# One product for y of a half chunk over v's tokens and the state's rows, in an RWKV-5 and SoLU feed-forward kernel

## The chip, the core and the metric

The kernel runs on one core of one Trainium2 chip. The metric is device time in microseconds (us); the kernel before takes 344.68 us (median of 3 runs, 343.82 to 345.14).

The core's engines have a queue each and run side by side, held together by semaphores: TensorE (PE: matmuls; PEld are its weight loads), VectorE (DVE), ScalarE (ACT), GpSimd (POOL), and SyncE (SP), which here issues nearly all DMAs. SBUF is the on-chip memory of 128 partitions, PSUM the accumulator memory that TensorE writes.

## The reference

```python
# attention: B=4, H=8, S=768, D=48, float32
for t in range(S):
    kt, vt, rt = (k[:, :, t], v[:, :, t], r[:, :, t])
    cur = np.einsum('bhd,bhe->bhde', u[None] * kt, vt)
    y[:, :, t] = np.einsum('bhd,bhde->bhe', rt, state + cur)
    state = w[None, :, :, None] * state + np.einsum('bhd,bhe->bhde', kt, vt)
# feed-forward: x is y as (3072 tokens, 384), d_ff = 1024
h = x @ w_in
e = np.exp(h - h_max); sm = e / (np.sum(e) + 1e-09); solu = h * sm
ln = (solu - mean) / np.sqrt(var + 1e-06) * g_ln
return ln @ w_out
```

The recurrence over tokens is computed in chunks. Within a chunk y is a masked product of scores (r against k, decayed) with v, plus a diagonal term (u), plus the product of r with the state carried in.

## The kernel before

A chunk is 128 tokens of one batch: 24 chunks, in the order batch fastest, so chunk i and chunk i+4 belong to the same batch. `direct_path` is written out by hand in the order in which every engine's instructions are issued; each engine runs its own in that order, and a later one can't pass an earlier one that waits. A general path behind a flag isn't run with these inputs.

Chunks 0 to 6 (`i < WHOLE`) are handled whole: `whole_scores`, `whole_y`, `whole_outer`. From chunk 7 on a chunk is cut in two halves of 64 tokens (`U`), and the main loop (`for i in range(LA + LO, ...)`) takes two chunks a turn; its first turn, i = 7, has an order of its own (`late`). In a turn with chunks i and i+1, and with the feed-forward of older chunks (ffn_in of j = i-2 and j+1, ffn_out of l = i-7 and l+1), TensorE's order is:

ffn_in(j), within(i, i+1), ffn_out(l), carried(i), carried(i+1), ffn_in(j+1), ffn_out(l+1), scores(i+2, i+3), outer(i+2, i+3).

The pieces that the change and the prediction touch:

- `diagonal` (L729): ScalarE writes for each of 8 heads the unit matrix times the diagonal term into AT; `take_scores` (L788): VectorE copies the masked scores over it, per chunk 2 instructions of 128x256.
- `scores` (L781) into two PSUM banks, `outer` (L880) into two buffers of the PSUM pool psM, which has four; psM also serves o_ps of ffn_out (L1016) and y_ps of the whole chunks.
- `within` (L843): y from AT and v, 32 products of 64 rows x 32 columns a chunk, into the two score banks. `carried` (L854) adds r times the state (first half) or times the state in mid chunk (second half), 24 products of 128 rows x 32 columns a chunk. The profile counts each float32 product twice, as two records.
- `take_y` (L864): ScalarE copies y out of PSUM into xT, the operand of ffn_in (L926) of the same chunk, which runs in the next turn.
- `middle` (L898): VectorE makes the state in mid chunk. `update` (L910, L914): VectorE adds the second half's outer product, GpSimd multiplies by the decay.
- `ffn_in` (L926) writes h into the one buffer of psH; ScalarE takes exp (L931); `unit` has VectorE's reciprocal (L937) and product solu (L939), which releases h, and ScalarE's identity (L941) and square (L942).
- `halve_ln` (L977), `halve_k` (L989), `halve_r` (L994): copies that split 32-bit words into halves, so that a transposing DMA on SP's queue (L966) can turn them; `join_ln` and `join_rk` (both L971) are VectorE's copies that put the words together again as lnT and rk.
- `decay_k`, `decay_r`, `weigh` (L697, L704, L710, L711): GpSimd's preparation of k, r and the diagonal term; `sum_own` (L715) is VectorE's sum for the latter.
- `check_next`: ScalarE's mag (L563) and VectorE's least (L565), a check of one piece of the weights a turn.
- `load`: k, r and v by three DMAs of SP a chunk (L472).

Of the kernel before, what the change touches and what calls it, by code (L numbers as in the profile page):

```python
# [399 lines left out]
def direct_path(  # L400
# [29 lines left out]
    nc = tc.nc  # L430
# [35 lines left out]
    kpads = [const.tile([128, H, P], F32, name=f"kpad{i}") for i in range(NLD)]  # L466
    vts = [const.tile([128, H, D + 32], F32, name=f"vt{i}") for i in range(NV)]
    def load(i, which="krv"):
        b, c = units[i]
        for t, src, n in ((kpads, k, "k"), (rpads, r, "r"), (vts, v, "v")):  # L470
            if n in which:
                nc.sync.dma_start(out=t[i % len(t)][:, :, 0:D],  # L472
                                  in_=src[b, :, ts(c, T), :].rearrange("h s d -> s h d"))


# [15 lines left out]

    banks = [psA.tile([128, HP * T], F32, name=f"at{q}") for q in range(2)]
    for ps in banks:
# [102 lines left out]
    for vt in vts:  # L596
        nc.gpsimd.memset(vt[:, :, D:], 0.0)
    neg_half = const.tile([128, 1], F32, name="neg_half")
    nc.gpsimd.memset(neg_half, -0.5)


    states = [const.tile([128, HP, 2, D], F32, name=f"state{b}") for b in range(B)]
    for St in states:
        nc.scalar.activation(out=St.rearrange("p a q d -> p (a q d)"),
                             in_=ident[:, 0:1].to_broadcast([128, dm]), func=ACT.Copy, scale=0.0)

    mids = [const.tile([128, HP, 2, D], F32, name=f"mid{n}") for n in range(2)]
    for St in mids:
        nc.scalar.activation(out=St.rearrange("p a q d -> p (a q d)"),
                             in_=ident[:, 0:1].to_broadcast([128, dm]), func=ACT.Copy, scale=0.0)  # L610

# [99 lines left out]
    def sum_own(i):  # L713
        own = live[i]["own"] = small.tile([128, H, 1], F32, name="own")
        nc.vector.tensor_reduce(out=own[:, :, 0], in_=live[i]["rku"], axis=AX.X, op=ALU.add)  # L715

    def diagonal(i):
        X = live[i]
        if i < WHOLE:
            AT, unit_matrix = apool.tile([128, H, T], F32, name="AT", bufs=3), ident  # L720
        else:

            if (i - WHOLE) % 2 == 0:
                X["ATs"] = apool.tile([128, 2, H, U], F32, name="AT", bufs=3)
                live.setdefault(i + 1, {})["ATs"] = X["ATs"]
            AT, unit_matrix = X["ATs"][:, (i - WHOLE) % 2], same
        X["AT"] = AT
        for h in range(H):
            nc.scalar.activation(out=AT[:, h, :], in_=unit_matrix, func=ACT.Copy, scale=X["own"][:, h])  # L729

    def factors(i):
        X = live.setdefault(i, {})
        X["rk"] = apool.tile([128, 2, HP, T], F32, name="rk", bufs=3)
        X["rT"], X["kT"] = X["rk"][:, 0], X["rk"][:, 1]
        return X

    def turn_r(i):
# [31 lines left out]
    def scores(chunks):  # L769
        chunks = [i for i in chunks if i < N]  # L770
        if not chunks:
            return
        ps = [t.rearrange("p (n a t) -> p n a t", n=2, t=U) for t in banks]
        for n, i in enumerate(chunks):
            X = live[i]
            X["scores"] = [ps[q][:, n] for q in range(2)]
            for a in range(HP):
                for c in range(2):
                    for q in range(2):
                        rows = slice(q * P, q * P + D)  # L780
                        nc.tensor.matmul(X["scores"][q][ts(c, U), a, :], X["kT"][rows, a, ts(c, U)],  # L781
                                         X["rT"][rows, a, ts(c, U)], start=True, stop=True)

    def take_scores(i):
        A4 = live[i]["AT"].rearrange("p (a q) t -> p a q t", q=2)
        mask = later if i < WHOLE else later_half
        for q in range(2):
            nc.vector.copy_predicated(A4[:, :, q, :], mask.to_broadcast([128, HP, mask.shape[2]]),  # L788
                                      live[i]["scores"][q])

    def parts(m):

        a, n = divmod(m, 3)
        at = {0: [(0, 0)], 1: [(0, 32), (1, 64)], 2: [(1, 96)]}[n]
        return [(2 * a + q, a * 2 * (D + 32) + off) for q, off in at]

# [5 lines left out]
    def whole_y(i):  # L805
        b, c = units[i]
        X = live[i]
        vt, AT, St = vts[i % NV], X["AT"], states[b]
        vf = vt.rearrange("p h d -> p (h d)")
        y_ps = psM.tile([128, KD, 128], F32, tag="m", name="y_ps")  # L810
# [17 lines left out]

    def within(chunks):
        chunks = [i for i in chunks if i < N]  # L830
        if not chunks:
            return
        opened = set()
        for n, i in enumerate(chunks):
            live[i]["y"] = [t[:, 0 : 2 * KD * U].rearrange("p (n j t) -> p n j t", n=2, t=U)[:, n]
                            for t in banks]
        for i in chunks:
            X = live[i]
            vf, AT = vts[i % NV].rearrange("p h d -> p (h d)"), X["AT"]
            for n, (m, h, at) in enumerate(inner):  # L840
                j, g = divmod(m, 4)
                for c in range(2):
                    nc.tensor.matmul(X["y"][c][ts(g, 32), j, :], vf[ts(c, U), at : at + 32],  # L843
                                     AT[ts(c, U), h, :], start=(g not in opened), stop=False,
                                     skip_group_check=True)
                opened.add(g)

    def carried(i):
        X = live[i]
        for c, St in enumerate((states[units[i][0]], X["mid"])):  # L850
            for m in range(12):
                a, n = divmod(m, 3)
                j, g = divmod(m, 4)
                nc.tensor.matmul(X["y"][c][ts(g, 32), j, :],  # L854
                                 St[:, a].rearrange("p q d -> p (q d)")[:, ts(n, 32)],
                                 X["rT"][:, a, ts(c, U)], start=False, stop=True,
                                 skip_group_check=True)

# [7 lines left out]
    def outer(chunks):  # L866
# [6 lines left out]
        for n, i in enumerate(chunks):  # L873
            X, vt = live[i], vts[i % NV]
            X["kv"] = [kv[c][:, n] for c in range(1 if units[i][1] == C - 1 else 2)]
            for a in range(HP):
                for q in range(2):
                    h = 2 * a + q
                    for c, dst in enumerate(X["kv"]):
                        nc.tensor.matmul(dst[q * P : q * P + D, a], X["kp"][ts(c, U), h, 0:D],  # L880
                                         vt[ts(c, U), h, 0:D], start=True, stop=True)

    def whole_outer(i):
        X, vt = live[i], vts[i % NV]
        X["kv"] = psM.tile([128, HP, D], F32, tag="m", name="kv_ps")
        for a in range(HP):
            for g in range(4):
                h = 2 * a + g // 2
                nc.tensor.matmul(X["kv"][ts(g, 32), a], X["kp"][:, h, ts(g % 2, 32)],
                                 vt[:, h, 0:D], start=True, stop=True)  # L890

    def middle(i):

        X, St = live[i], states[units[i][0]]
        X["mid"] = mids[i % 2]
        for q in range(2):
            rows = slice(q * P, q * P + D)
            nc.vector.tensor_add(X["mid"][rows, :, q], X["kv"][0][rows], St[rows, :, q])  # L898

    def update(i):  # L900
        b, c = units[i]
        if c == C - 1:
            return
        X, St = live[i], states[b]
        for q in range(2):
            rows = slice(q * P, q * P + D)
            wT = pw[rows, 0, 7].unsqueeze(2).to_broadcast([D, HP, D])
            S = St[rows, :, q]
            if i >= WHOLE:
                nc.vector.tensor_add(S, X["kv"][1][rows], X["mid"][rows, :, q])  # L910
            elif c > 0:
                nc.vector.tensor_add(S, X["kv"][rows], S)
            if i >= WHOLE or c > 0:
                nc.gpsimd.tensor_mul(S, S, wT)  # L914
            else:
                nc.vector.tensor_mul(S, X["kv"][rows], wT)

# [188 lines left out]


    todo = list(range(6, len(pieces)))
    now = []
# [70 lines left out]
    for i in range(LA + LO, N + LA + LO, 2):  # L1180
# [10 lines left out]
        if late:  # L1191
# [8 lines left out]
            load(i + 3, "v")  # L1200
            load(i + 4, "v")
        decay(i + 4)
        for n in (j - 2, j - 1):
# [14 lines left out]
        if j < N and not late:  # L1218
            ffn_in(j)
            unit(j)  # L1220
            within([i, i + 1])
        if second_pair:
# [5 lines left out]
        if late:  # L1228
            load(i + 6, "kr")
            within([i, i + 1])  # L1230
            ffn_in(j + 1)
            halve_rk(i + 4)
            load(i + 7, "kr")
        for n in (i, i + 1):
            if n < N:
                carried(n)
        if l + 3 < N:
            halve_ln(l + 3)
        for n in (i, i + 1):
            if n < N:  # L1240
                take_y(n)
        for n in (i, i + 1):
# [10 lines left out]
        if j + 1 < N and not late:  # L1253
            unit(j + 1)
        ffn_out(l + 1)
        halve_rk(i + 5)
        for n in (i + 4, i + 5):
            if n < N:
                sum_own(n)
        attend([i + 2, i + 3])  # L1260
        if l + 2 < N:
# [46 lines left out]
```

## Time and profile before

| | us |
|---|---|
| median of 3 runs | 344.68 (343.82 to 345.14) |
| span of the profiled execution | 343.8 |
| ffn_in, L926, 288 records | 130.5 busy |
| ffn_out, L1016, 400 records | 128.3 busy |
| within, L843, 1088 records | 12.8 busy |
| carried, L854, 816 records | 17.8 busy (9.0 + 8.8) |
| scores, L781, 544 records | 10.0 busy |
| outer, L880, 480 records | 7.9 busy |
| diagonal of the half chunks, L729, 136 instructions | 34.2 busy, ScalarE |

A busy time is the time in which at least one instruction of the group runs; the mean of one record is longer than its share, since records overlap. A turn of the main loop is the time between two starts of L781: 148.36, 174.33, 200.27, 226.21 and 252.16 us from the span's start, 26.0 us each.

### The profile page before, as it was taken

What the parts mean: (1) busy time and instruction counts of PE and PEld (TensorE: products, weight loads), DVE (VectorE), ACT (ScalarE), POOL (GpSimd) and SP (SyncE); (2) the same over time, 40 slices, a digit from 0 to 9 for tenths busy, and PEclk for the clock granted to TensorE, in tenths of its full rate; (3) what the DMA queues carried; (4) which work ended last, traced back from release to release, by engine and by line L of the source; (5) the groups of instructions that cost most, each with busy time, mean ns of one, the idle gap of its engine ahead of it and who ended that gap; (6) DMA issues with size and microseconds to landing.
All of it is one profiled execution on the core that took longest, in us unless ns stands there. A gap on an engine that the chain in (4) does not pass through costs nothing.

```text
span 343.8 us, 10628 instructions
## 1 busy us (share of the span) xinstructions
PE 333.2 (97%) x4483; PEld 198.7 (58%) x4483; DVE 209.1 (61%) x379; ACT 234.5 (68%) x477; POOL 176.2 (51%) x202
## 2 busy tenths in 40 slices
PE   8989999999999999999999999999999999999993
PEld 6846666655555456556556555555555555555563
DVE  8786988789766386586576577575365052332410
ACT  4866887997970977985794794796594466456510
POOL 7789887699999198585683683630300000000000
PEclk9999999999999999999999999999999999999999
DMA  6989998299999999999969959849942433454541
GB/s 147 249 228 240 246 216 131 55 126 178 188 183 178 159 210 192 194 190 172 193 127 175 213 107 154 206 92 153 191 105 38 122 88 81 94 130 109 135 100 36
DMA packets 164742, 52.69 MB, mean 153 GB/s; under 512 B 157901, under 2 KB 161102, under 8 KB 164686
## 3 DMA queue, kind: packets, MB, share of 16 engines
q1 hardware_dynamic: 164684, 51.92, 79.4%
q8 instruction: 37, 0.61, 0.8%
q14 instruction: 19, 0.16, 0.2%
q10 hardware_dynamic: 2, 0.00, 0.0%
HBM read 26.75 MB, written 4.72 MB: 92 GB/s over the span
## 4 chain that ended last, share of the span: by engine, by line
PE 87%; DMA 4%; SPq 3%; DVE 3%; POOL 1%; issue 0%; ACT 0%; DVEq 0%; POOLq 0%
PE h_ps L926 35%; PE o_ps L1016 35%; PE at L854 3%; PE at L843 3%; PE at L781 3%; DMA raw<-in_moe_w_in_dram 2%; PE y_ps L815 2%; SPq L472 2%; DMA halves<-halves 2%; PE kv_ps L880 2%; SPq L511 1%; PE at L764 1%; PE tr_ps L741 1%; PE tk_ps L749 1%; POOL w_in_sb L545 1%; DVE rk L971 1%
## 5 line engine op out<-in xcount | busy, mean ns | idle before, releaser
L926 PE MATMUL h_ps<-w_in_sb,xT 128*128 128x512 f32 x288 | 130.5, 601 | 1.9 <-DVE solu L939 0.9
L1016 PE MATMUL o_ps<-w_out_sb,lnT 128*128 128x384 f32 (+1 forms) x400 | 128.3, 476 | 0.0
L1016 PEld LDWEIGHTS o_ps<-w_out_sb,lnT 128*128 128x128 f32 x400 | 74.3, 190 | 48.9 <-issue 4.3
L926 PEld LDWEIGHTS h_ps<-w_in_sb,xT 128*128 128x128 f32 x288 | 52.6, 190 | 62.4 <-issue 56.3
L931 ACT ACTIVATE e<-h_ps 128x1024 f32<-128x1024 f32 x24 | 24.6, 1025 | 41.7 <-PE h_ps L926 41.6
L941 ACT ACTIVATE solu<-solu,st 128x1024 f32<-128x1024 f32 x24 | 27.5, 1147 | 30.8 <-DVE solu L939 30.8
L914 POOL TENSOR_TENSOR state<-state,pw 48x192 f32<-48x192 f32 x32 | 23.2, 724 | 47.4 <-DVE state L910 45.5
L977 ACT COPY halves<-solu 128x2048 uint16<-128x2048 uint16 x24 | 45.3, 1889 | 2.2 <-DMA halves<-halves 2.2
L971 DVE COPY lnT<-halves 128x2048 uint16<-128x2048 uint16 x24 | 38.0, 1595 | 12.1 <-DMA halves<-halves 11.8
L948 POOL TENSOR_SCALAR st<-st 128x1 f32<-128x1 f32 x24 | 5.6, 234 | 64.2 <-ACT e L942 64.1
L710 POOL TENSOR_TENSOR rku<-kpad,u_bc 128x384 f32<-128x384 f32 x24 | 31.9, 1329 | 8.7 <-DVE own L715 7.9
L729 ACT ACTIVATE AT<-same,own 128x64 f32<-128x64 f32 x136 | 34.2, 337 | 0.0
L697 POOL TENSOR_TENSOR kp<-kpad,kdec 128x512 f32<-128x512 f32 x24 | 31.8, 1327 | 3.0 <-ACT kdec L646 1.4
L939 DVE SCALAR_TENSOR_TENSOR solu<-h_ps,st,e 128x1024 f32<-128x1024 f32 x24 | 30.8, 1284 | 2.0
L711 POOL TENSOR_TENSOR rku<-rku,rpad 128x384 f32<-128x384 f32 x24 | 30.3, 1262 | 1.9
L565 DVE TENSOR_REDUCE least<-mag 128x1 f32<-128x384 f32 (+1 forms) x14 | 8.5, 606 | 36.9 <-ACT mag L563 36.9
L937 DVE RECIPROCAL st<-sums 128x1 f32<-128x1 f32 x24 | 3.8, 158 | 40.0 <-ACT e L931 39.6
L1018 ACT ACTIVATE o<-o_ps,st 128x384 f32<-128x384 f32 (+1 forms) x25 | 13.9, 558 | 18.5 <-PE o_ps L1016 12.6
L942 ACT ACTIVATE e<-solu 128x1024 f32<-128x1024 f32 x24 | 25.4, 1057 | 0.8
L971 DVE COPY rk<-halves 128x2048 uint16<-128x2048 uint16 x15 | 25.2, 1683 | 0.2
L704 POOL TENSOR_TENSOR rp<-rpad,rdec 128x512 f32<-128x512 f32 x15 | 22.7, 1512 | 0.4 <-DMA rpad<-in_r_dram 0.4
L788 DVE COPY_PREDICATED AT<-later_half,at 128x256 f32<-128x256 uint32 x34 | 12.5, 437 | 15.4 <-PE at L781 15.0
(105 smaller groups left out, 388.6 us busy)
## 6 DMA issues: line engine op xcount, KB each, us to landing
raw<-in_moe_w_in_dram SPq DMA_DIRECT2D x12, 512.0 KB, 5.4
raw<-in_moe_w_out_dram SPq DMA_DIRECT2D x16, 384.0 KB, 4.2
kpad<-in_k_dram SPq DMA_DIRECT2D x24, 192.0 KB, 4.8
rpad<-in_r_dram SPq DMA_DIRECT2D x24, 192.0 KB, 5.2
vt<-in_v_dram SPq DMA_DIRECT2D x24, 192.0 KB, 5.2
out_dram<-o SPq DMA_DIRECT2D x23, 192.0 KB, 3.3
halves<-halves SPq DMA_TRANSPOSE x39, 5.1
out_dram<-o SPq DMA_DIRECT2D x2, 96.0 KB, 2.5
```

The lines of the kernel that those rows point to most:

```text
L697: nc.gpsimd.tensor_mul(X["kp"].rearrange("p h d -> p (h d)"), kpads[i % NLD].rearrange("p h d -> p (h d)"), kdec.rearrange("p a d -> p (a ...
L710: engine.tensor_mul(rku, kpads[i % NLD][:, :, 0:D], u_bc)
L711: engine.tensor_mul(rku, rku, rpads[i % NLD][:, :, 0:D])
L729: nc.scalar.activation(out=AT[:, h, :], in_=unit_matrix, func=ACT.Copy, scale=X["own"][:, h])
L926: nc.tensor.matmul(h_ps[:, ts(n, NX)], X["xT"][:, j, :], w_in_sb[:, j, ts(n, NX)], start=(j == 0), stop=(j == KD - 1))
L931: nc.scalar.activation(out=e, in_=h_ps, func=ACT.Exp, accum_out=sums[:, i : i + 1])
L939: nc.vector.scalar_tensor_tensor(out=solu, in0=X["h"], scalar=rs, in1=X["e"], op0=ALU.mult, op1=ALU.mult, accum_out=tot)
L941: nc.scalar.activation(out=solu, in_=solu, func=ACT.Identity, scale=-float(dff), bias=tot)
L942: nc.scalar.activation(out=X["e"], in_=solu, func=ACT.Square, accum_out=ss)
L971: nc.vector.tensor_copy(out=words.bitcast(U16).rearrange("p n (t o) -> p o n t", o=2), in_=turned)
L977: nc.scalar.copy(out=both.rearrange("p (o n) -> p o n", o=2), in_=split(X["solu"]))
L1016: nc.tensor.matmul(o_ps, X["lnT"][:, f, :], w_out_sb[:, f, part], start=(f == 0), stop=(f == KF - 1))
```

## The change

From chunk 7 on, y of a half chunk is one set of products instead of two. The contracted rows of a product are now the 64 tokens of the half and the 48 rows of the state together. So v and the state stand in one tile (`vts[...][:, c]`), and the scores and the turned r in another (`G`):

- first half: rows 0 to 63 are v's tokens, 64 to 111 the state; second half: rows 64 to 127 are v's tokens, 0 to 47 the state in mid chunk, 32 to 63 set to zero beforehand.
- v is loaded by two DMAs a chunk, one for each half; `middle` and `update` write the state straight into the v tiles, and GpSimd's decay product is one of 48x384 instead of two of 48x192.
- `diagonal` goes from ScalarE to VectorE, two instructions of 64x512; `take_scores` is two of 64x512 for a chunk.
- `place`, new, copies the turned r beside the scores: four ScalarE copies of 48x256 a chunk.
- `merged_y` takes the place of `within` and `carried`, 32 products a chunk, and writes into psM. It and take_y now stand at the end of the turn, after ffn_out(l+1), before the next scores.
- twelve memsets go to GpSimd ahead of the loop over the last whole chunks; AT and rk share six tiles (`bigs`), and the states of the whole chunks share the place of two other tiles.

TensorE's order in a turn becomes: ffn_in(j), ffn_out(l), ffn_in(j+1), ffn_out(l+1), merged_y(i), merged_y(i+1), scores(i+2, i+3), outer(i+2, i+3). ScalarE's order in the same turn becomes: halve_ln, exp(j), identity, square, halve_k, mag, o, place(i+2), halve_ln, exp(j+1), identity, square, place(i+3), o, halve_k, take_y(i), take_y(i+1).

```diff
+        if "v" in which:
+            vt = vts[i % NV]
+            for n, at, size in ((0, 0, T),) if i < WHOLE else ((0, 0, U), (1, U, U)):
+                nc.sync.dma_start(
+                    out=vt[at : at + size, n, :, 0:D],
+                    in_=v[b, :, ds(c * T + at, size), :].rearrange("h s d -> s h d"))
...
     def diagonal(i):
...
+        G = X["G"] = merged(i)
+        if i < WHOLE + 4:
+            nc.gpsimd.memset(G[32:64, 1], 0.0)
+        for c in range(2):
+            rows = ts(c, U)
+            nc.vector.tensor_mul(
+                G[rows, c].rearrange("p a q u -> p (a q) u"),
+                same[rows].unsqueeze(1).to_broadcast([U, H, U]),
+                X["own"][rows].to_broadcast([U, H, U]))
...
+    def place(i):
+
+        X = live[i]
+        for q in range(2):
+            rows = slice(q * P, q * P + D)
+            nc.scalar.copy(out=X["G"][P : P + D, 0, :, q, :], in_=X["rT"][rows, :, 0:U])
+            nc.scalar.copy(out=X["G"][0:D, 1, :, q, :], in_=X["rT"][rows, :, U:T])
...
+        for c in range(2):
+            rows = ts(c, U)
+            nc.vector.copy_predicated(
+                X["G"][rows, c].rearrange("p a q u -> p q a u"),
+                later_half[rows].unsqueeze(1).to_broadcast([U, 2, HP, U]),
+                X["scores_both"][rows])
...
-    def within(chunks):
...
+    def merged_y(i):
+        X = live[i]
+        y_ps = psM.tile([128, KD, 128], F32, tag="m", name="y_ps")
         opened = set()
...
+        for c, rows in ((0, slice(0, P + D)), (1, slice(0, 128))):
+            vf = vts[i % NV][rows, c].rearrange("p h x -> p (h x)")
             for n, (m, h, at) in enumerate(inner):
                 j, g = divmod(m, 4)
...
+                nc.tensor.matmul(y_ps[ts(g, 32), j, ts(c, U)], vf[:, at : at + 32],
+                                 X["G"][rows, c, h // 2, h % 2, :], start=(g not in opened),
+                                 stop=last[m] == n, skip_group_check=True)
                 opened.add(g)
...
-    def carried(i):
...
+        if i >= WHOLE or c > 0:
+            S = vts[(i + B) % NV][P : P + D, 0, :, 0:D]
+            nc.gpsimd.tensor_mul(S, S, wide[P : P + D].unsqueeze(2).to_broadcast([D, H, D]))
...
+    for vt in vts:
+        nc.gpsimd.memset(vt[:, 1, :, D:], 0.0)
+        nc.gpsimd.memset(vt[32:64, 1], 0.0)
...
-            within([i, i + 1])
...
-        for n in (i, i + 1):
-            if n < N:
-                carried(n)
+        for n in first:
+            place(n)
         if l + 3 < N:
             halve_ln(l + 3)
-        for n in (i, i + 1):
-            if n < N:
-                take_y(n)
...
+        for n in second:
+            place(n)
         ffn_out(l + 1)
         halve_rk(i + 5)
...
+        for n in (i, i + 1):
+            if n < N:
+                merged_y(n)
+                take_y(n)
         attend([i + 2, i + 3])
```

## The prediction

> **What bounds the kernel now.** I read the page's busy table, then the windows by stage, then the timeline.
>
> ```profile
> PE 333.2 (97%) x4483; PEld 198.7 (58%) x4483; DVE 209.1 (61%) x379; ACT 234.5 (68%) x477; POOL 176.2 (51%) x202
> PE 87%; DMA 4%; SPq 3%; DVE 3%; POOL 1%; issue 0%; ACT 0%; DVEq 0%; POOLq 0%
> ```
> ```profile
> 90.00:116.00 26.00, 25.07 (x418) 14.59 (x407) 16.00 (x24) 16.18 (x34) 20.05 (x20) 1.00 1.21 183
> 194.00:220.00 26.00, 26.00 (x409) 14.88 (x408) 17.19 (x27) 18.50 (x38) 15.54 (x17) 1.00 0.82 155
> ```
> Columns of the second: sum, then busy PE, PEld, DVE, ACT, POOL, clock, DMA. One turn of the main loop (two chunks) takes 26.0 us, and TensorE fills all of it at full clock. So a product taken off TensorE is worth its time, if the others keep up. Whether they do is read from the timeline of one turn:
>
> ```profile
> 200.27 1.16 PE L781 MATMUL at<-rk 48*64 48x64 f32 x64
> 201.48 1.44 DVE L788 COPY_PREDICATED AT<-later_half,at 128x256 f32<-128x256 uint32 x4 [1.97 <-PE at L781]
> 204.30 4.19 DVE L971 COPY lnT<-halves 128x2048 uint16<-128x2048 uint16 x2
> 211.95 1.15 ACT L941 ACTIVATE solu<-solu,st 128x1024 f32<-128x1024 f32 x1 [3.22 <-DVE solu L939]
> 216.27 1.89 ACT L977 COPY halves<-solu 128x2048 uint16<-128x2048 uint16 x1
> 218.06 0.98 ACT L864 COPY xT<-at 128x192 f32<-128x192 f32 x4
> 220.95 5.32 PE L1016 MATMUL o_ps<-w_out_sb,lnT 128*128 128x384 f32 x16
> ```
> Here xT leaves PSUM (L864) in mid turn, at 218.06; the product that needs it (ffn_in, L926) starts at about 228.0. That is 9 us of cover. The second place to see is the one where TensorE already stalls:
>
> ```profile
> 106.33 2.02 DVE L971 COPY lnT<-halves 128x2048 uint16<-128x2048 uint16 x1 [5.11 <-DMA halves<-halves]
> 111.84 1.15 ACT L941 ACTIVATE solu<-solu,st 128x1024 f32<-128x1024 f32 x1 [7.94 <-DVE solu L939]
> 111.86 5.42 PE L926 MATMUL h_ps<-w_in_sb,xT 128*128 128x512 f32 x12 [0.93 <-DVE solu L939]
> 119.73 0.95 ACT L864 COPY xT<-at 128x192 f32<-128x192 f32 x4
> 120.58 1.04 ACT L931 ACTIVATE e<-h_ps 128x1024 f32<-128x1024 f32 x1
> 124.20 5.42 PE L926 MATMUL h_ps<-w_in_sb,xT 128*128 128x512 f32 x12
> ```
> A transposing DMA holds back lnT, VectorE's queue holds back solu behind it, and ffn_in(8) starts only when solu(7) has released the single h buffer.
>
> **What the Trainium skill says.** "TensorEngine Tiling (Array Packing)", Available Configurations: 64x32 tiles make eight, 128x32 tiles four. The trace agrees in kind: `within` (64x32) takes 1.42 us for 128 records (11 ns each), `carried` (128x32) 1.48 us for 96 (15 ns). "SBUF — State Buffer", Who interferes with whom: a VectorE instruction with two SBUF inputs, and a 2-port copy, exclude GpSimd reads for the whole instruction. The trace agrees for the copies: L971 takes 1.3 us alone and up to 2.4 beside GpSimd, L710 1.0 or 2.0. "VectorE: DVE Perf Modes", Two Vector instructions with no wait between them: an instruction on another start quadrant is held until the earlier one ended. L788 (same rows) starts every 0.335 us though one lasts 0.437; L898, which alternates quadrants, starts every 0.37 and lasts 0.352. Agrees.
>
> **Part by part.**
> *Products.* A turn loses 128+96 records (1.42+1.48 = 2.90 us) and gets 128 records of 112 or 128 rows by 32 columns. Inside `carried`, 24 records take 0.33 us, 13.8 ns each; 128 of them are 1.77, plus 0.16 of drain, 1.93 us. Gain 0.97 us per turn on TensorE, 8.2 us for the 17 chunks; bounds 1.2 (no drain) and 0.6 (15.4 ns and a drain for each half).
>
> *Diagonal.* ScalarE loses 8 instructions of a chunk (2.0 us). VectorE gets two fp32 tensor_tensor of 64x512: L742 with 512 elements takes 0.69, and the alternating halves don't overlap, so 1.4 us a chunk; up to 3 if GpSimd holds the port.
> *Masked copies.* 4 of 256 elements (1.34 us a pair) become 4 of 512, held: 0.727 each (L788's other form), 2.9 us. +1.55.
> *place.* Four ScalarE copies of 48x256 a chunk. No row of this shape; ScalarE starts every 0.25 us at 64 to 192 elements and 0.45 at 384, so I take 0.33 (bounds 0.26, 0.40): 1.3 us a chunk.
> *Update.* GpSimd: 2 of 48x384 for 4 of 48x192, 2 us both ways. The wait of the update on `carried` goes (2.0 us once), VectorE is late there anyway.
> *Early memsets.* Twelve on GpSimd after weigh(4), 0.2 and 0.5 each by L597's 0.3 for 256: 4.2 us, 1.0 of it in the wait at 35 us. kp(5) is then ready at 39.7; TensorE asks for it at 48.1, GpSimd has caught up by 56. Cost 0; at most 2 if that cover goes.
> *v in two halves.* One issue more a chunk on SP, before two transposes: +0.1 to 0.4 us a turn; those are wanted half a turn later. Taken 0.
> *psM.* y takes two of its four buffers a turn, so the second kv buffer waits for o(l+1)'s eviction.
>
> *The moved y.* merged_y and take_y now stand at the end of a turn, before the scores, and ffn_in of the next turn needs xT 1.85 us after the scores' start (scores 0.95, outer 0.9) instead of 9 us later. In ScalarE's queue take_y stands behind exp(j+1), identity, square, place, o's eviction and halve_k.
>
> Turn with the scores' start as 0. VectorE: 1.2, masks 2.9, mid 1.5, lnT 1.25, diagonal 1.4, lnT 1.25, rk 1.25: 10.8; reciprocal, solu, ScalarE's L941 at about 12.35 (before: 211.95-200.27 = 11.7). ScalarE from there to exp(j+1): identity and square 2.24, halve_k 0.94, mag 0.68, o 0.46, place 1.32, halve_ln 1.79: 7.43, so 19.8; TensorE offers h at 18.0. From exp: solu and L941 2.93, square end 2.23, place 1.32, o 0.46, halve_k 0.94, take_y 0.46, signal 0.15: 8.5. xT at 28.3. With a turn of 25.0 it is wanted at 26.85: a stall of 1.4. The stall delays the next scores as well and gives the others that much, so turns alternate, 25.0 and 26.4. If VectorE's second rk and diagonal meet GpSimd's state products (they start within 1 us), up to 1.6 more, 27.9. Four turns (13 to 19; the last without its halve_k and own sums, 0.95 less): 101.8 to 104.8, against 103.8 now (148.36 to 252.16): -2.0 to +1.0.
>
> *Where it starts, chunks 7 to 12.* solu(7) stays bound by the transposes in SP's queue: ffn_in(8) again near 112, 0.2 to 0.8 later. Before, the y products of 7 to 10 filled TensorE's wait before it; now 9 and 10 come after it. ScalarE: L941(7) at 111.84 to 112.6, then two halve_ln, halve_k, mag, o and place: 9.2, exp(8) at 121.0 to 121.8; +8.5: xT(9) at 129.6 to 130.3, where ffn_in(9) stood at 124.20. From there 5.3 x 4 of feed-forward and 1.93: scores(13) at 152.7 to 153.4, now 148.36: +4.3 to +5.1.
>
> *End.* Chunks 21, 22: -0.97; chunk 23: -0.5.
> Sum: 4.7 (-0.4/+0.4), -0.5 (-1.5/+1.5), -1.5: +2.7, say +2.5 (it could be +0.8 to +4.6). The span of 343.8 lies 0.9 under the median of 344.68 (runs from 343.82 to 345.14); I add to the median: 347.2 us.
>
> **Rivals.**
> 1. *TensorE stays the bound* (not slower). Queues stretch, ScalarE has 1.4 us a chunk less to do and catches up by chunk 9; only the first stage's wait is kept. Gain 6 x 0.97 + 0.5 = 6.3: 338.4 us. For it: TensorE at 100% in eight windows of 26 us, ScalarE at 71% in the one shown. Against: the order of take_y above, which no average shows. 10%.
> 2. *An even exchange*: the stall at 124 comes to 2 us less (place at 0.26, solu(7) a little earlier) and turns alternate at 25.0 and 26.2: 344.5 us. 25%.
> 3. *VectorE becomes the bound*, one mechanism: diagonal and lnT copies wait for GpSimd's port in each of the turns 9 to 19, 1 to 2 us a turn. It decides once VectorE's first half reaches 12.5 us instead of 10.8, since solu then arrives after ffn_in(j+1) is due at 12.45 and everything behind shifts: turns of 27.2, 347.2 + 4 x 1.3 = 352.4 us. For it: 4.19 us for two lnT in the turn shown. Against: GpSimd's part ends sooner there, since its own-sum wait ends sooner. 12%.
> 4. The merged products run no faster than the two that they replace: 0.97 more in the turn of 9 and 10, 1.9 in the four alternating ones (half is hidden in the stalls), 1.5 at the end: 347.2 + 4.4 = 351.6 us. 3%.
> The forecast has 50%.
>
> **How the numbers follow.** Range 342.5 to 351.5: the forecast's own (345.5 to 349.3) widened over rival 2 and towards 3. Under half a per cent is what a measurement of this kernel can tell from no change: 343.0 to 346.4. Faster: rival 1 and a fifth of 2, with a little of the forecast's lower tail, 0.14. Same: most of 2 and the forecast's lower part, 0.26. Slower 0.60.
>
> **What would show it.** Right: y records of 14 ns, 1.8 to 2.0 us a turn; ScalarE's take_y last before a stall of ffn_in (L926's line) of 3 us or more near 124 to 130 us, with waits on ACT xT; after it alternating stalls near 1 us; scores(13) near 153. Wrong: ffn_in never waits for xT, turns of 25.0 us (rival 1); VectorE solu named as the releaser of ffn_in(j+1) in each turn (rival 3); TensorE idle before 70 us because of kp (the memsets). I would be wrong most easily in the place copies' 0.33 us and in who holds the shared port.

## The result, and the profile after

The changed kernel takes 368.83 us (median of 4 runs, 367.67 to 370.07) against 344.91 us for the kernel before, measured beside it: a ratio of 1.069, 95% interval 1.066 to 1.073. The direction of the forecast (slower) was right, its size far too small: 347.2 us was named, with a range that ended at 351.5. The profiled execution of the changed kernel took 368.47 us, its span is 366.7.

The page of the changed kernel, its busy table, the shares of the chain that ended last, and three groups (busy us, mean ns, idle time before them):

```profile
PE 331.6 (90%) x3667; PEld 197.0 (54%) x3667; DVE 255.2 (70%) x415; ACT 228.9 (62%) x389; POOL 179.6 (49%) x202
...
PE 49%; DVE 22%; ACT 9%; issue 6%; POOL 6%; DMA 4%; SPq 1%; POOLq 0%; DVEq 0%; ACTq 0%
...
L931 POOL TENSOR_TENSOR vt<-vt,wide 48x384 f32<-48x384 f32 x16 | 21.2, 1342 | 65.2 <-DVE vt L928 64.9
...
L738 DVE TENSOR_TENSOR big<-same,own 64x512 f32<-64x512 f32 x34 | 40.5, 1190 | 0.3
...
L816 DVE COPY_PREDICATED big<-later_half,at 64x512 f32<-64x512 uint32 x34 | 24.9, 734 | 17.1 <-PE at L803 16.7
```

TensorE still does nearly the same work, but the span grew by 22.8 us and its share fell from 97% to 90%. In the chain its share fell from 87% to 49%; VectorE (3% before) has 22%, ScalarE (0% before) 9%. The masked copies (L816) cost what was predicted, 0.73 us each. The diagonal (L738) has a mean of 1190 ns; its instructions range from 671 to 1678 ns, with a median of 1302.

Two turns of the main loop in windows (sum, then busy PE, PEld, DVE, ACT, POOL with counts, clock, DMA share, GB/s):

```profile
161.70:188.90 27.20, 24.88 (x320) 14.31 (x312) 22.06 (x30) 17.38 (x28) 14.82 (x14) 1.00 0.95 156
188.90:218.50 29.60, 26.66 (x324) 14.93 (x316) 23.55 (x33) 19.55 (x32) 16.47 (x16) 0.94 0.92 143
```

Before, every such turn was 26.0 us with TensorE busy throughout and VectorE for 14.7 to 18.9 us (17.2 in the turn that the prediction shows). Now a turn of 27.2 and one of 29.6 alternate, TensorE has holes of 2.3 and 2.9 us, VectorE is busy for 22 to 24 us, and in the longer turn the clock that TensorE was granted is below full speed (0.94). The timeline (start, us, engine, line, operation, count, in brackets the idle time before and what ended it) shows a hole of the first turns, then the loop that sets the length of the later ones:

```profile
99.22 1.16 PE L803 MATMUL at<-big 48*64 48x64 f32 x64
...
105.24 1.53 PE L891 MATMUL kv_ps<-vt,kp 64*48 64x48 f32 x62 [4.79 <-ACT o L1033]
...
106.70 6.71 PE L941 MATMUL h_ps<-w_in_sb,xT 128*128 128x512 f32 x12
...
161.71 1.16 PE L803 MATMUL at<-big 48*64 48x64 f32 x64
...
164.87 0.93 PE L891 MATMUL kv_ps<-vt,kp 64*48 64x48 f32 x62 [1.93 <-ACT o L1033]
...
169.11 2.88 DVE L738 TENSOR_TENSOR big<-same,own 64x512 f32<-64x512 f32 x2
...
174.41 0.15 DVE L952 RECIPROCAL st<-sums 128x1 f32<-128x1 f32 x1
...
176.00 1.15 ACT L956 ACTIVATE solu<-solu,st 128x1024 f32<-128x1024 f32 x1 [3.18 <-DVE solu L954]
...
176.60 5.31 PE L941 MATMUL h_ps<-w_in_sb,xT 128*128 128x512 f32 x12
...
181.53 2.67 POOL L931 TENSOR_TENSOR vt<-vt,wide 48x384 f32<-48x384 f32 x2 [10.09 <-DVE vt L928]
...
183.44 2.99 DVE L738 TENSOR_TENSOR big<-same,own 64x512 f32<-64x512 f32 x2
183.88 1.02 ACT L946 ACTIVATE e<-h_ps 128x1024 f32<-128x1024 f32 x1
...
186.46 0.16 DVE L952 RECIPROCAL st<-sums 128x1 f32<-128x1 f32 x1
...
187.00 2.00 PE L864 MATMUL y_ps<-big,vt 112*32 112x64 f32 x128
...
188.05 1.15 ACT L956 ACTIVATE solu<-solu,st 128x1024 f32<-128x1024 f32 x1 [3.06 <-DVE solu L954]
...
188.93 1.16 PE L803 MATMUL at<-big 48*64 48x64 f32 x64
...
192.08 0.58 ACT L1033 ACTIVATE o<-o_ps,st 128x384 f32<-128x384 f32 x1
...
192.71 0.93 PE L891 MATMUL kv_ps<-vt,kp 64*48 64x48 f32 x62 [2.55 <-ACT o L1033]
...
193.49 0.86 ACT L875 COPY xT<-y_ps 128x384 f32<-128x384 f32 x2
...
194.03 7.11 PE L941 MATMUL h_ps<-w_in_sb,xT 128*128 128x512 f32 x12 [0.39 <-ACT xT L875]
```

The loop runs from the scores at 161.71 over VectorE (masks, state, lnT, diagonal, lnT, rk, reciprocal) to ScalarE's identity at 176.00, through ScalarE's queue to exp(j+1) at 183.88, through VectorE once more, where the second pair of diagonals stands before the reciprocal, and through ScalarE's queue to take_y (L875) and ffn_in at 194.03. That is 32.3 us; the prediction had 28.3. VectorE's second pair of diagonals takes 2.99 us while GpSimd multiplies the states (L931, to 184.20) and then prepares k (L703, from 184.28): exp starts at 183.88 and is done about 1 us later, but the reciprocal follows only at 186.46.

Where the 22.8 us arose: scores(13) start at 161.71 instead of 148.39 (given as 148.36 above; +13.3), the four turns from there to scores(21) take 112.4 instead of 103.8 (+8.6), and the rest to the end of the span 92.5 instead of 91.7 (+0.9).

### The profile page after: what moved, and what is told of

Its sections match the earlier page's. It is cut to its first block, busy times and chain, and to the rows that moved or that the text cites. A ratio compares the mean times of both kernels' runs of the same rounds, so it can differ in the third digit from the quotient of the medians.

```text
span 366.7 us, 8996 instructions
## 1 busy us (share of the span) xinstructions
PE 331.6 (90%) x3667; PEld 197.0 (54%) x3667; DVE 255.2 (70%) x415; ACT 228.9 (62%) x389; POOL 179.6 (49%) x202
## 4 chain that ended last, share of the span: by engine, by line
PE 49%; DVE 22%; ACT 9%; issue 6%; POOL 6%; DMA 4%; SPq 1%; POOLq 0%; DVEq 0%; ACTq 0%
PE o_ps L1031 21%; PE h_ps L941 20%; DVE big L738 5%; DVE big L816 3%; DMA halves<-halves 3%; DVE big L986 3%; DVE lnT L986 3%; PE y_ps L864 2%; DVE solu L954 2%; ACT solu L956 2%; POOL kp L703 2%; DVE vt L912 2%; ACT halves L1004 2%; ACT halves L992 2%; DVE vt L928 1%
## 5 line engine op out<-in xcount | busy, mean ns | idle before, releaser
L941 PE MATMUL h_ps<-w_in_sb,xT 128*128 128x512 f32 x288 | 134.8, 618 | 6.9 <-DVE solu L954 4.8
L941 PEld LDWEIGHTS h_ps<-w_in_sb,xT 128*128 128x128 f32 x288 | 55.2, 197 | 72.6 <-issue 66.3
L931 POOL TENSOR_TENSOR vt<-vt,wide 48x384 f32<-48x384 f32 x16 | 21.2, 1342 | 65.2 <-DVE vt L928 64.9
L738 DVE TENSOR_TENSOR big<-same,own 64x512 f32<-64x512 f32 x34 | 40.5, 1190 | 0.3
L986 DVE COPY lnT<-halves 128x2048 uint16<-128x2048 uint16 x24 | 34.4, 1431 | 7.9 <-DMA halves<-halves 7.4
L703 POOL TENSOR_TENSOR kp<-kpad,kdec 128x512 f32<-128x512 f32 x24 | 33.9, 1412 | 7.9 <-PE kv_ps L891 2.4
L816 DVE COPY_PREDICATED big<-later_half,at 64x512 f32<-64x512 uint32 x34 | 24.9, 734 | 17.1 <-PE at L803 16.7
L716 POOL TENSOR_TENSOR rku<-kpad,u_bc 128x384 f32<-128x384 f32 x24 | 28.3, 1179 | 9.3 <-DVE own L721 8.0
L717 POOL TENSOR_TENSOR rku<-rku,rpad 128x384 f32<-128x384 f32 x24 | 27.2, 1135 | 1.9
L891 PE MATMUL kv_ps<-vt,kp 64*48 64x48 f32 x480 | 10.8, 226 | 13.9 <-ACT o L1033 13.9
L986 DVE COPY big<-halves 128x2048 uint16<-128x2048 uint16 x15 | 21.2, 1411 | 0.3
```

What stands on the lines that cost most here:

```text
L703: nc.gpsimd.tensor_mul(X["kp"].rearrange("p h d -> p (h d)"), kpads[i % NLD].rearrange("p h d -> p (h d)"), kdec.rearrange("p a d -> p (a ...
L716: engine.tensor_mul(rku, kpads[i % NLD][:, :, 0:D], u_bc)
L717: engine.tensor_mul(rku, rku, rpads[i % NLD][:, :, 0:D])
L738: nc.vector.tensor_mul(G[rows, c].rearrange("p a q u -> p (a q) u"), same[rows].unsqueeze(1).to_broadcast([U, H, U]), X["own"][rows].to_br ...
L816: nc.vector.copy_predicated(X["G"][rows, c].rearrange("p a q u -> p q a u"), later_half[rows].unsqueeze(1).to_broadcast([U, 2, HP, U]), X[ ...
L941: nc.tensor.matmul(h_ps[:, ts(n, NX)], X["xT"][:, j, :], w_in_sb[:, j, ts(n, NX)], start=(j == 0), stop=(j == KD - 1))
```

## The experiments

The theory after the result was: two things add up. y at the end of a turn makes xT late, since take_y is the last of ScalarE's queue; and the diagonal makes VectorE late, longer than forecast because GpSimd works beside it. The rival explanations were one of the two alone. The experiments take away each, then both, and then look for another place for the diagonal. For each, the table gives the median, the ratio to the kernel before on the same chip with its interval, and where its profiled execution gained or lost against the one of before (scores(13), four turns, rest, in us). The last three columns come from one execution each. Their sum lies within 1.4 us of what the medians differ by, except in c (1.9 us too low), b (2.3 too low) and i (4.0 too low).

| kernel | us | ratio (95%) | to scores(13) | four turns | rest |
|---|---|---|---|---|---|
| the change | 368.83 | 1.069 (1.066 to 1.073) | +13.3 | +8.6 | +0.9 |
| a: y in mid turn | 356.01 | 1.031 (1.027 to 1.035) | +9.1 | +2.7 | -1.6 |
| b: diagonal is a memset (its term left out) | 357.16 | 1.036 (1.033 to 1.040) | +9.8 | -0.1 | +0.7 |
| c: second place behind y | 360.69 | 1.047 (1.042 to 1.053) | +10.4 | +3.8 | +0.1 |
| d: before, diagonal on VectorE | 348.51 | 1.010 (1.007 to 1.013) | +3.0 | 0.0 | +0.5 |
| e: a and b | 345.84 | 1.001 (1.000 to 1.003) | +3.9 | -2.5 | -1.7 |
| f: a, diagonal on GpSimd | 355.46 | 1.029 (1.026 to 1.031) | +14.1 | -2.7 | -1.6 |
| g: f, second place last | 355.16 | 1.026 (1.022 to 1.030) | +13.7 | -2.8 | -0.8 |
| h: b and c | 353.94 | 1.024 (1.021 to 1.026) | +9.7 | -0.8 | +0.7 |
| i: a, diagonal on ScalarE, then GpSimd | 348.82 | 1.014 (1.011 to 1.018) | +4.8 | -3.1 | -1.5 |
| j: a, diagonal on ScalarE | 349.22 | 1.010 (1.007 to 1.014) | +7.6 | -2.3 | -1.6 |
| k: the change, diagonal as in i | 359.69 | 1.042 (1.040 to 1.045) | +12.5 | +1.2 | +0.5 |

**y back in mid turn (a).** merged_y before the first place, take_y after halve_ln(l+3), nothing else:

```diff
-        for n in (i, i + 1):
-            if n < N:
-                merged_y(n)
-                take_y(n)
...
+        for n in (i, i + 1):
+            if n < N:
+                merged_y(n)
         for n in first:
             place(n)
         if l + 3 < N:
             halve_ln(l + 3)
+        for n in (i, i + 1):
+            if n < N:
+                take_y(n)
```

> The changed kernel with merged_y and take_y back in mid turn, where carried and take_y stood before. Theory of place (the moved y closes a loop of ScalarE, TensorE and PSUM at the end of each turn): the waits of outer on o's eviction and of ffn_in on xT go, turns come to 25.0 to 26.5 us, 338 to 347 us in all. Theory of VectorE (its diagonal, held up by GpSimd's port, makes solu late): solu still arrives late in each turn, 355 us or more.

Measured: 12.8 us less than the change, at the lower edge of what was set for the theory of VectorE; but the waits on o and xT have gone too, as the theory of place said. Its turns are still long. In the one shown the clock is 1.00, and VectorE is busy for 23.1 of 27.0 us, a larger share than in the turns of the change above (a turn of kernel a in windows):

```profile
183.20:210.20 27.00, 25.05 (x313) 13.99 (x312) 23.11 (x32) 17.88 (x28) 15.59 (x15) 1.00 0.95 156
```

So the place of y explains about half of the loss. With y in mid turn the chain of xT is gone, and VectorE is what remains late: its reciprocal for exp(j) comes 15.0 us after the scores (183.16 to 198.13).

**The diagonal taken away (b).** VectorE's product becomes a memset of the same 64x512. It still takes 0.485 us, where the product had a mean of 1.19, so VectorE is relieved of a part only:

```diff
-            nc.vector.tensor_mul(
-                G[rows, c].rearrange("p a q u -> p (a q) u"),
-                same[rows].unsqueeze(1).to_broadcast([U, H, U]),
-                X["own"][rows].to_broadcast([U, H, U]))
+            nc.vector.memset(G[rows, c].rearrange("p a q u -> p (a q u)"), 0.0)
```

> The changed kernel with VectorE's diagonal product replaced by a memset of the same 64x512 tiles: the diagonal term of chunks 7 to 23 is left out. Theory of place: VectorE's two stretches get 0.7 to 2 us shorter each, turns about 1.5 to 2 us shorter but still ended by xT, 350 to 357 us. Theory of VectorE: nothing is late any more, 338 to 346 us.

Measured: 11.7 us less than the change, just over the range for the theory of place (350 to 357) and far from 338 to 346. The four turns are at 25.7 to 26.4 us, as long as the forecast's mean of 25.7 (it had 25.0 and 26.4 by turns). So the forecast's reckoning of the turn was about right for a VectorE that isn't late; most of what it missed there is the diagonal.

**The second place out of the way (c).** `for n in second: place(n)` moves from before ffn_out(l+1) to behind the take_y of the same turn:

```diff
-        for n in second:
-            place(n)
         ffn_out(l + 1)
...
                 take_y(n)
+        for n in second:
+            place(n)
```

> The changed kernel with the second chunk's four place copies issued after take_y instead of before o's eviction. Theory of place: o and xT come 1.66 us earlier in each of eight turns; the loop spans two turns, so 0.8 to 1.7 us a turn, 355 to 362 us. Theory of VectorE: no change, 366 to 370 us.

Measured: 8.1 us less than the change, within the range for the theory of place. Nothing is left out, four copies of ScalarE only stand behind take_y instead of before it. That is the evidence that ScalarE's queue ahead of take_y is part of the path.

**The diagonal alone, in the kernel before (d).**

```diff
         X["AT"] = AT
+        if i >= WHOLE:
+            for c in range(2):
+                rows = ts(c, U)
+                nc.vector.tensor_mul(AT[rows], same[rows].unsqueeze(1).to_broadcast([U, H, U]),
+                                     X["own"][rows].to_broadcast([U, H, U]))
+            return
         for h in range(H):
```

> The kernel before with one part of the change alone: the diagonal of chunks 7 to 23 made by VectorE, two products of 64x512 a chunk, instead of eight ScalarE instructions. Theory of place: TensorE still covers it, 344 to 348 us. Theory of VectorE: solu late in each turn, 352 us or more.

Measured: +4.0 us, half a us over the range for the theory of place, and by its profile nearly all of it at the start: scores(7) come at 78.28 instead of 74.67, and from scores(13) to scores(21) nothing changes. With the old products and short masks VectorE has room in these turns, and the diagonal is hidden. A rival that calls the diagonal dear in every turn by itself fails here; dear at the start it is. In a, whose y stands in mid turn as here, longer masks and the place copies are added, among other parts of the change, and the four turns lose 2.7 us; which of these takes the room wasn't tried apart.

**Both undone (e).** The edits of a and b together.

> y in mid turn and the diagonal of chunks 7 to 23 a memset (the diagonal term is left out). If the two causes are separate (the place of y, and VectorE's time under GpSimd's port), both gains show: TensorE is the bound again, turns near 25.0 us, 337 to 342 us. If VectorE's masked copies and ScalarE's place copies alone keep the loop long: 345 to 352 us.

Measured: no difference from before can be told (20 runs against 23). At 345.84 us the expectation of 337 to 342 for two separate causes was missed, and the number lies in the range set for the other branch. But that branch spoke of a loop that stays long, and in the profile the four turns are 25.1 to 25.5 us, shorter than before. Here the gain of the merged products is seen at last, in the four turns and the rest: -2.5 and -1.7 us. The first stage takes it back: +3.9, of which the memset's remaining time may be a part. A turn of kernel e in windows:

```profile
177.70:203.00 25.30, 24.99 (x316) 13.98 (x315) 20.03 (x32) 17.89 (x28) 15.01 (x14) 1.00 1.05 172
```

**The diagonal on GpSimd (f), and place last as well (g).** f is a with `nc.gpsimd.tensor_mul` in place of `nc.vector.tensor_mul` in the diagonal; g is f with the second place at the end of the turn.

```diff
-            nc.vector.tensor_mul(
+            nc.gpsimd.tensor_mul(
```

> y in mid turn and the diagonal of chunks 7 to 23 made by GpSimd, two products of 64x512 a chunk, nothing left out. GpSimd gets 4 x 1.3 us a turn more. If it was VectorE's queue that the diagonal blocked: 340 to 346 us. If the shared port is the bound, whoever asks: 350 to 356 us, no better than with the diagonal on VectorE.

> As the run before, with the second chunk's place copies issued last in the turn, behind o's eviction and halve_k. If ScalarE's queue still counts (o's eviction, halve_k and halve_ln wait behind four copies of 0.41 us), 1 to 4 us less than without it. If only VectorE and GpSimd count, the same within 1 us.

Measured: 355.5 and 355.2 us. f's number lies in the range for the shared port as the bound, but not for that reason: the four turns gain 2.7 and 2.8 us with nothing left out, as they should where the diagonal blocked VectorE's queue, and the first stage loses as much as in the change. The timeline of f shows the hole, in the turn of chunk 7:

```profile
91.41 7.95 PE L941 MATMUL h_ps<-w_in_sb,xT 128*128 128x512 f32 x12 [8.35 <-DVE solu L954]
```

VectorE's masks wait 5.4 us for GpSimd's diagonal there, which stands behind GpSimd's preparation of k and r, and solu stands behind the masks. That place(second) doesn't matter in g (within 1 us of f) is what the theory wants: take_y is no longer behind it.

**Diagonal gone and place behind y, y still at the end (h).** The edits of b and c.

> y at the end of the turn as in the change, but with the diagonal a memset (its term left out) and the second chunk's place copies behind take_y. If the place of y does harm by itself: 348 us or more. If it does harm only behind a long ScalarE and VectorE queue: 339 to 346 us.

Measured: 353.94 us, 3.2 less than b, and in the range set for a place of y that does harm by itself. In the first stage it is as slow as b (+9.7), with outer waiting 3.13 us for o's eviction until 100.78. Clearing VectorE and shortening ScalarE's queue isn't enough there.

**The diagonal on ScalarE at first, then on GpSimd (i); on ScalarE throughout (j); and i's diagonal with y at the end (k).** For chunks below 13 (in j all):

```diff
+        if i < 13:
+            for h in range(H):
+                nc.scalar.activation(out=G[:, :, h // 2, h % 2, :],
+                                     in_=same.unsqueeze(1).to_broadcast([128, 2, U]),
+                                     func=ACT.Copy, scale=X["own"][:, h])
+            return
```

> y in mid turn; the diagonal of chunks 7 to 12 made by ScalarE (8 instructions of 128x128 a chunk, over both halves' columns), of later chunks by GpSimd; nothing left out. The runs with y in mid turn and GpSimd's diagonal had turns of 25.0 to 25.7 us from the fourth on, and lost their time in the first three turns, where GpSimd is full. If that is all, the first three turns come to about 75 us as before and the whole to 340 to 344 us. If ScalarE's 2.4 us a chunk more delays the first turns as much: 347 us or more.

> As the run before, but the diagonal by ScalarE throughout. ScalarE then has about 22 us of work in a turn, VectorE and GpSimd as little as in the run with the memset. If only VectorE and the port mattered: 342 to 346 us. If ScalarE's queue with the place copies is a bound of its own: turns above 25.5 us, 347 to 352 us.

> As the first of these three, but y at the end of the turn as in the change. If the place of y harms by itself, 8 to 14 us more than with y in mid turn, with waits of outer on o and of ffn_in on xT. If it harms only behind a late VectorE: within 3 us of it.

Measured: i and j at 349 us are the fastest versions with the merged products that leave nothing out, and still slower than before, by 1.4 and 1.0%; which of them is faster can't be told. Both missed the better of their two ranges. i's first three turns, from scores(7) to scores(13), took 78.8 us and not 75, and j's turns came to 25.5 us. The profiled execution of i was the fastest of its runs (345.85 us against the median of 348.82), so its three columns flatter it by some 3 us. With the change, a, k and i, the four corners of "y where" and "diagonal where" are there: 368.8, 356.0, 359.7 and 348.8 us. Moving y costs 12.8 with the diagonal on VectorE and 10.9 without; the diagonal on VectorE costs 9.1 with y at the end and 7.2 in mid turn. Two causes that nearly add; neither alone explains the loss. At 10.9 us more than i, k fell in the range for a place of y that harms by itself. It shows the first cause without the second; what TensorE waited for (us in total, times, longest):

```profile
PE kv_ps L895 <- ACT o L1037: 11.0, 5, 7.8
```

Of these 11.0 us, 7.8 are one wait at the end of the turn of chunks 7 and 8: y has taken two buffers of psM, and outer(9, 10) gets its second one only when ScalarE's queue, which in k holds diagonals too, reaches o's eviction. In the first stage k therefore gains little on the change (+12.5 against +13.3); what it gains lies in the four turns, +1.2 instead of +8.6.

## Why the prediction was wrong

**What was right.** y's products take 2.00 us a turn (1.93 predicted), the masked copies 0.73 us each, and the path over ScalarE's queue to take_y with its alternating turns is in the trace as told. In i's profiled execution (its fastest), where little delays TensorE, the four turns last 25.0 to 25.2 us, 0.7 to 0.9 less than before: nearly all of the predicted 0.97 is there. In e, whose profiled execution lies near its median, they last 25.1 to 25.5. (The bound of 1.2 for no drain should read 1.1: 2.90 less 1.77.)

**The step that failed** is "Turn with the scores' start as 0", by which xT was to come at 28.3 and the stall to be 1.4 us. Counted from the scores at 161.71, ffn_in has its xT at 32.3. The difference of 4.0 is made of terms:

- *The diagonal at 1.4 us a chunk.* Measured 2.88 at 169.11 and 2.99 at 183.44. The first delays the reciprocal (12.7 after the scores instead of 10.8, together with 0.4 more for lnT, which also ran beside GpSimd). The second, not in the sum at all between exp and solu, makes exp to identity 4.17 us instead of 2.93. Together 2.7 to 2.8 of the 4.0. The Trainium skill, "SBUF — State Buffer", Who interferes with whom, which the prediction quoted, says that a product with two SBUF inputs and GpSimd's reads exclude each other; the trace now agrees. Of the 34 instructions ten took 671 to 690 ns, and one of these has a GpSimd product of 384 or 512 columns beside it; the other 24 took 846 to 1678 ns, and all of them have one. The prediction gave "up to 3 if GpSimd holds the port" and "up to 1.6 more" as upper bounds and summed the lower ones.
- *place at 0.33 us.* Measured 0.40, one every 0.415 us. The first place takes 0.35 us more ahead of exp(j+1), the second place the same ahead of take_y: 0.7.
- The remaining half microsecond lies in the lnT copy and in small gaps.

The forecast had turns with no stall and with 1.4 us by turns. With xT 4.0 us later TensorE's holes are 2.3 us (1.93 for outer, which waits for o, and 0.39 for xT) and 2.9 us (2.55 and 0.39). o's eviction and take_y stand close behind each other in ScalarE's queue, and no run here was made to move one of the two waits without the other, so they aren't told apart. The longer one was followed by a second cost that no term covered, the clock (below): 1.7 us in the turn from 188.93. So 25.0 and 2.3 make 27.3 (the turn took 27.2), and 25.0, 2.9 and 1.7 make 29.6 (29.5). The four turns: -2.0 to +1.0 predicted, +8.6 measured. The prediction's upper bounds for the diagonal were right, and its sum took the lower ones.

**The first stage** was to cost +4.3 to +5.1 and cost +13.3. Two waits are missing. The diagonal of chunk 7 stands on VectorE before a solu for which TensorE then waits (1.77 us before 71.58 us); scores(7) come 2.2 us later than before, 3.6 in d, where the wait is 2.73 us and a slow ffn_in of 7.08 follows. The prediction charged nothing for it. And the wait of outer for o's eviction was named ("psM") but not priced: 4.79 us before 105.24, of which ScalarE's queue is the cause (halve_ln, identity, square, place and only then o, all in a row from 98.78). Two slow ffn_in of this stage (below) took 2.4 us more. A full sum of the stage was not worked out. With y in mid turn and no diagonal on VectorE the first stage costs +3.9 in e and +4.8 in i (its fastest execution; +7.6 in j), about the forecast's figure, which was computed for the late y. That nearness is chance: what is left in e and i is of another cause. In e ffn_in waits for solu, which stands behind an lnT copy that a transposing DMA released at 108.93 (before: 106.33); why the transposes come later wasn't tried and stays open.

**The end** was to give 1.5 and took 0.9. All versions with y in mid turn give 1.5 to 1.7 there (g 0.8), all with y at the end lose 0.1 to 0.9: the gain was right, and the moved y takes it.

**The rivals.** Rival 3, VectorE as the bound with 352.4 us, is true in its first half: diagonal and lnT take longer beside GpSimd, and VectorE's first half reaches its mark of 12.5 us (12.7). But its sign is missing: ffn_in(j+1) at 176.60 waits for no solu, since ffn_in(j) came late as well. VectorE's lateness goes on over ScalarE's queue to xT. So it comes on top of the forecast's path and not in its place, and its time should have been added to the forecast. Rivals 1 and 2 fell: ffn_in does wait for xT, and turns are no 25 us. Rival 4 fell with y's 2.00 us. The twelve memsets on GpSimd were taken at nothing. TensorE has one new wait for kp, 1.08 us before 40.05; but i, which keeps the memsets and has the same wait of 1.08 us, before 39.33, has its scores(7) at 74.40, no later than the 74.67 of before, so they cost nothing that lasts to there.

## What to carry to other kernels

An instruction moved behind a long queue of another engine must be priced over the whole loop that returns to it, with each engine's instructions at their durations beside the others; the shortest duration in the trace is the price without company. Where two theories of a loss act on the same loop at different places, add them: a rival isn't an alternative to the forecast unless one excludes the other. And when the bound engine gains 1 us a turn, work moved onto an engine with 9 us of idle time can still cost more, because it stands ahead of the one instruction for which the loop waits.

## What was not expected of the hardware

After some pauses TensorE runs slower for a while, and it is the next large products that take longer. The changed kernel in windows, TensorE alone (span, busy PE, clock, DMA share, GB/s):

```profile
162.00:166.00 4.00, 1.87 (x124) 1.00 0.09 31
166.00:171.50 5.50, 5.32 (x13) 1.00 1.02 155
189.90:194.00 4.10, 1.19 (x79) 1.00 0.12 43
194.00:201.00 7.00, 6.97 (x13) 0.76 1.05 174
```

After a pause of 1.93 us (at 162.94 to 164.87) ffn_in has the full clock and takes 5.42 us; after 2.55 us, with only short outer products in between, the clock is 0.76 and it takes 7.11. The kernel before has no such slow ffn_in. In the changed kernel there are four, at 106.70, 137.90, 194.03 and 250.10 (6.71, 6.47, 7.11 and 6.70 us), together 5.4 us above 5.4 each, nearly a quarter of the loss if nothing covered them. The Trainium skill, "TensorE: Matmul & The Clock Gate", What's actually happening, says that TensorE's clock is halved after an idle window of about 3.4 us and comes back after as long a busy one, the window running free. The size agrees here: half speed for 3.4 of 7.0 us would be a mean of (1.7 + 3.6) / 7.0 = 0.76, an estimate from that page's figure; measured is 0.76. Elsewhere it is larger: in j an ffn_out (5.3 to 5.4 us otherwise) took 8.26 at a mean clock of 0.65.

The length of the pause doesn't agree, and it doesn't decide by itself: 2.55 us sufficed in the changed kernel at 192.71. At the same place of the program 2.66 us did not suffice in the changed kernel and 2.65 us did in a:

```profile
86.81 5.39 PE L941 MATMUL h_ps<-w_in_sb,xT 128*128 128x512 f32 x12 [2.66 <-DVE solu L954]
...
86.20 7.08 PE L941 MATMUL h_ps<-w_in_sb,xT 128*128 128x512 f32 x12 [2.65 <-DVE solu L954]
```

In a, too, a pause of 1.93 us before 137.98 was followed by an ffn_out of 7.09, and in i one of 3.19 us before 109.27 by none that was slow. A window that runs free would make such a mixture, but no run here shows where it begins, so the threshold stays open. A stall can thus cost more than its own length: in the four cases of the changed kernel 1.1 to 1.7 us more.
